# A gated linear recurrence in chunks: the state kept every 64 tokens, with key-value products as 64x64 tiles

## Chip, cores and metric

The kernel runs on one core of a Trainium2 chip. Its time is the device time of one execution in microseconds (us); a run is repeated and the median counts. The engines are named as in the profile: PE (TensorE, matrix products), PEld (its weight loads), DVE (VectorE), ACT (ScalarE), POOL (GpSimd) and SP (SyncE, which issues most transfers).

## What is computed

Two blocks in a row. The first is a recurrence over 768 tokens, for 4 batches and 8 heads of 48 channels; the decay of each step is a complex number per channel. The second mixes the tokens with a product of rank 32 and then applies a two-layer network with a residual.

```python
mag = np.sqrt(a_re * a_re + a_im * a_im)
scale = np.minimum(mag, 0.999) / (mag + 1e-06)
a_re_n, a_im_n = a_re * scale, a_im * scale
for t in range(S):
    new_re = ar * S_re - ai * S_im
    new_im = ar * S_im + ai * S_re
    S_re, S_im = new_re + kv, new_im        # kv: outer product of k and v at t
    y[:, :, t] = einsum('bhd,bhde->bhe', q[:, :, t], S_re)
# x: y as (4, 768, 384)
u = x + (x^T @ U @ V)^T
out = u + np.maximum(u @ w_ch1, 0) @ w_ch2
```

All inputs and outputs are float32.

## The kernel before

The tokens of a batch are cut into 6 chunks of 128 (`CH`), 24 chunks in all. A chunk goes through these stages.

*Gates* (`gates`, L506 to L631), for groups of one or two chunks: the logarithm of the decay's size and its angle, from ACT's functions and some DVE steps. Sums over tokens are products with constant matrices (`es ps` L552, `ph` L610). `totals` (L557) makes the decays over spans of 4 to 128 tokens, and four transfers per group copy them from the tile `E` into the tile `T`, real rows at 0 to 47 and imaginary rows at 48 to 95 (`D2` = 96). `T_of(i, n)` (L633) picks the spans of n tokens.

*Preparation* (`prep`, L639): queries and keys are weighted and turned by their angles into `qkc`, with real and imaginary parts side by side (96 columns a head). PE transposes each head (`tr`, L660) and ACT copies the results into `QK`, so that the 96 channels lie on partitions and the tokens along the row.

*Levels* (`chain`, L668): the product of keys and queries within a chunk is needed with its decay. It is built from small tiles: three rounds of `inner` on blocks of 32 tokens (L694), whose results are kept by mask in `DG` (L700) and placed by four small transfers into the diagonal of `AT` (L731). Between rounds `times` and `grow` (L704, L716) multiply parts of `QK` by the decay of ever longer spans. After `grow` by 16 the `corners` (L743) fill the 32x32 tiles beside the diagonal of each 64 tokens, after `grow` by 32 the `corner` (L760) fills the one 64x64 tile beyond. `AT` is 128 keys by 128 queries a head.

*Rest of a chunk*: `grow` by 64 (L767) brings queries and keys to the edges of the chunk; keys are transposed back into `ks` (L780), except in a batch's last chunk. `outputs` (L789) adds, per head, values times `AT` (L794, all 128 keys deep) and the state `G` of the chunk before times the queries (L798), in a PSUM bank `yT`. `state` (L807) multiplies `ks` by the values (`dk`, L809, one product a head with 96 wide weights); DVE makes the new `G` from the old one, the decay over 128 tokens and `dk` (L813 to L817). `yT` goes through ACT, a transpose `yr` (L824) and ACT again into `xo`.

*Mixing* (`mixer`, L831), two chunks at a time, once all six chunks of the batch are there: `rank`, `mixed`, the first layer `up` (L880) and the second layer `down` (L904, L947).

All operations are handed to a class `Plan` with an engine, an assumed cost, a rank and the buffers they need. `Plan.order` lets them run in a simple model, and the order that comes out is the order of the instructions on each engine. The ranks come from the table `URGENCY` (L25), one number for each kind of work and chunk; smaller goes first, and the mixing goes last where anything else is ready. A `way` marks PE operations that divide the array alike, so that they are kept together. Where PE has nothing to do in the model and no mixing has started, a product without use is issued (`spare`, L1067). The engines run their instructions in order, so a wait on PE holds all that is queued behind it.

PSUM has four pools of two banks: A (`inner`, `corners`, `corner`, `ks ps`), T (sums and `tr`), Y (`yT`, `dk`, `yr`) and M (`up`, `down`). Chunks from the group `PAIRED` = 6 on go through their levels in pairs (`together`, L1009).

## Time and profile before

| | |
|---|---|
| median of 3 runs | 729.14 us (724.9 to 730.22) |
| span of the profiled execution | 722.6 us |
| PE busy | 706.3 us, of which `spare` 57.4 |
| `up`, 864 records | 196.1 us busy |
| `down` by the windows (union of all forms) | 178.1 us |
| VectorE busy | 484.1 us, of which `QK` growths (144) 169.6 |
| ScalarE busy | 399.1 us |
| first `up` starts at | 143.3 us |

How to read it. Times of groups are sums of the durations of their instructions, and matmuls overlap: two that follow each other closely are both counted as busy for part of the same time. The windows view takes the union of the durations, so its sums are lower. What a matmul costs in a row of many is read from the distance of two starts in the timeline. A float32 product leaves two records,[...] and a transpose leaves one. "128*64" after an operation names the rows and columns of the array that it uses, and "128x128" the partitions and columns of the moving operand.

### The profile page before, as it was taken

The page shows a single profiled execution, that of the slowest core. Times are in us where ns is not written, and L with a number is a line of the kernel's source. Part 1 is how long each engine was busy: PE and PEld are TensorE (multiplying, and loading weights), DVE is VectorE, ACT ScalarE, POOL GpSimd, SP SyncE. Part 2 cuts the span into 40 slices and gives each one's busy share as a digit, 9 for nine tenths or more (in the row PEclk, how much of TensorE's full clock was granted, in tenths as well). Part 3 has the DMA queues.
Part 4 walks back from the last instruction along what each step waited for, and adds up shares of the span by engine and source line. Part 5 has one row for each costly group of instructions (what it writes and reads, how often), then busy time and mean ns, then how long its engine had stood idle before and what let it go on. Part 6 is the DMA issues. An engine that isn't in the chain of part 4 may idle for free.

```text
span 722.6 us, 23175 instructions
## 1 busy us (share of the span) xinstructions
PE 706.3 (98%) x10322; PEld 614.7 (85%) x10322; DVE 484.1 (67%) x732; ACT 399.1 (55%) x734; POOL 49.7 (7%) x91
## 2 busy tenths in 40 slices
PE   7899999999999999999999999999999999999998
PEld 7777888786788888978888888798898897989997
DVE  5899999787987958878587685384674741322313
ACT  6696986867789587659988636504314122010010
POOL 5010000010100100000010001000000000000000
PEclk9999999999999999999999999999999999999999
DMA  8787944777415332253441132211110000000000
GB/s 205 154 212 152 214 96 77 172 163 132 100 30 124 67 72 46 44 114 64 86 91 21 26 79 55 46 41 33 35 38 13 15 26 1 22 1 23 6 16 23
DMA packets 165251, 53.00 MB, mean 73 GB/s; under 512 B 154080, under 2 KB 160416, under 8 KB 165152
## 3 DMA queue, kind: packets, MB, share of 16 engines
q1 hardware_dynamic: 161072, 42.26, 27.2%
q0 software_dynamic: 4080, 9.27, 5.6%
q8 instruction: 81, 1.33, 0.8%
q14 instruction: 18, 0.15, 0.1%
HBM read 33.59 MB, written 4.72 MB: 53 GB/s over the span
## 4 chain that ended last, share of the span: by engine, by line
PE 74%; ACT 11%; DVE 10%; issue 2%; DMA 1%; SPq 0%; DVEq 0%; ACTq 0%
PE up L880 21%; PE down L947 19%; PE inner L694 5%; PE tr L660 5%; DVE QK L312 3%; PE yT L794 3%; PE dk L809 3%; ACT x L309 2%; PE down L904 2%; PE yT L798 2%; PE es ps L552 2%; PE mixed L861 2%; PE tot L578 2%; ACT y L309 1%; PE ks ps L780 1%
## 5 line engine op out<-in xcount | busy, mean ns | idle before, releaser
L880 PE MATMUL up<-uT,w 128*128 128x256 f32 x864 | 196.1, 382 | 0.0
L312 DVE TENSOR_TENSOR QK<-QK,T 96x1024 f32<-96x1024 f32 x144 | 169.6, 1186 | 16.7 <-PE corners L743 7.2
L880 PEld LDWEIGHTS up<-uT,w 128*128 128x128 f32 x864 | 161.3, 190 | 22.8 <-issue 0.8
L309 ACT ACTIVATE h<-up 128x512 f32<-128x512 f32 x72 | 42.7, 593 | 158.2 <-PE up L880 155.6
L947 PE MATMUL down<-w,h 128*128 128x192 f32 x396 | 71.8, 327 | 0.0
L947 PEld LDWEIGHTS down<-w,h 128*128 128x128 f32 x396 | 65.2, 190 | 3.3
L312 DVE TENSOR_TENSOR qkc<-qk,cs 128x768 f32<-128x768 f32 x48 | 45.8, 954 | 30.0 <-PE tr L660 24.5
L939 DVE TENSOR_TENSOR stage<-h 128x384 f32<-128x384 f32 x22 | 12.2, 555 | 75.9 <-ACT h L309 75.9
L1067 PE MATMUL spare<-ident 128*128 128x128 f32 x404 | 57.4, 288 | 2.5 <-POOL ident masks.py:199 1.5
L663 ACT COPY QK<-tr 96x512 f32<-96x512 f32 x96 | 52.1, 581 | 13.9 <-PE tr L660 13.7
L694 PEld LDWEIGHTS inner<-QK 96*32 96x32 f32 x4608 | 45.1, 109 | 16.2 <-issue 9.4
L1067 PEld LDWEIGHTS spare<-ident 128*128 128x128 f32 x404 | 51.3, 198 | 5.7 <-issue 1.9
L315 DVE TENSOR_TENSOR xo<-down,xo 128x192 f32<-128x192 f32 (+1 forms) x79 | 29.5, 385 | 38.2 <-PE down L947 38.2
L660 PE MATMUL tr<-ident,qkc 128*96 128x128 f32 x384 | 52.7, 275 | 2.0 <-DVE qkc L312 1.1
L694 PE MATMUL inner<-QK 96*32 96x16 f32 (+1 forms) x4608 | 50.7, 190 | 2.3 <-issue 1.7
L660 PEld LDWEIGHTS tr<-ident,qkc 128*96 128x96 f32 x384 | 41.3, 127 | 8.3 <-issue 1.8
L748 ACT COPY AT<-corners 32x128 f32<-32x128 f32 x96 | 24.5, 255 | 32.1 <-PE corners L743 31.0
L891 POOL DMA_DIRECT2D out_dram<-xo x32 | 17.9, 560 | 335.2 <-DVE xo L315 315.4
L794 PE MATMUL yT<-AT,VP 128*64 128x128 f32 x384 | 36.8, 279 | 0.0
L947 PE MATMUL down<-stage 128*128 128x192 f32 x198 | 36.4, 327 | 0.0
L700 DVE COPY_PREDICATED DG<-mask,inner 128x128 f32<-128x128 int32 (+1 forms) x72 | 24.2, 340 | 17.3 <-PE inner L694 14.0
L306 ACT ACT_TABLE_LOAD x26 | 33.4, 1283 | 1.2 <-PEq L1107 0.7
(116 smaller groups left out, 1106.1 us busy)
## 6 DMA issues: line engine op xcount, KB each, us to landing
stage<-in_moe_w_ch_dram SPq DMA_DIRECT2D x12, 768.0 KB, 5.0
ar<-in_a_re_dram SPq DMA_DIRECT2D x24, 192.0 KB, 3.4
ai<-in_a_im_dram SPq DMA_DIRECT2D x24, 192.0 KB, 3.4
qk<-in_q_dram SPq DMA_DIRECT2D x24, 192.0 KB, 3.8
qk<-in_k_dram SPq DMA_DIRECT2D x24, 192.0 KB, 4.9
VP<-in_v_dram SPq DMA_DIRECT2D x24, 192.0 KB, 3.7
w<-stage POOLq DMA_DIRECT2D x12, 384.0 KB, 7.0
T<-E SPq DMA_DIRECT2D x44, 96.0 KB, 3.0
```

Source lines behind the costliest of these rows:

```text
L306: ACT(1.37, rank, lambda: nc.scalar.preload_act_table_set(name), writes=[TABLE])
L309: return nc.scalar.activation(out=o, in_=i, func=f, **kw)
L312: nc.vector.tensor_tensor(out=o, in0=a, in1=b, op=OP.mult)
L315: nc.vector.tensor_tensor(out=o, in0=a, in1=b, op=OP.add)
L660: nc.tensor.transpose(out=get(*ps)[0:D2, j], in_=get(*qkc)[:, hh * HH + j].rearrange("p u d -> p (u d)"), identity=ident)
L663: ACT(c_act(HH * CH) - 0.05, R1, lambda u=u, hh=hh, ps=ps: nc.scalar.copy(out=get(*QK)[:, u, hh * HH:(hh + 1) * HH], in_=get(*ps)[0:D2]), ...
L694: nc.tensor.matmul(out=get(*ps)[js, h], lhsT=k_of(h)[:, js], rhs=part(q_of(h)[:, js], "p"), start=True, stop=True, tile_position=(0, j * BLK))
L748: ACT(0.32, RR, lambda r=r, u=u: nc.scalar.copy(out=get(*ATi).rearrange("p (a u) t -> p a u t", u=2)[r:r + BLK, :, u, r + BLK:r + 2 * BLK] ...
L794: nc.tensor.matmul(out=a[u * DP:(u + 1) * DP, p], lhsT=vv[:, h], rhs=get(*ATi)[:, h], start=True, stop=(c == 0), tile_position=(0, u * DP))
L880: nc.tensor.matmul(out=get(*ps)[:, e], lhsT=w1[:, f, (ff + e) * 128:(ff + e + 1) * 128], rhs=get(*uT)[:, f], start=(f == 0), stop=(f == KD ...
L947: nc.tensor.matmul(out=get(*to)[:, part], lhsT=x(j), rhs=y[:, j], start=(first and j == 0), stop=(j == KH - 1), skip_group_check=not first)
L1067: nc.tensor.matmul(out=spare[0], lhsT=ident, rhs=ident, start=True, stop=True)
```

## The change

A chunk of 128 tokens now carries its state across two halves of 64 (`HC`). What changes in the work:

- Real and imaginary rows lie 64 partitions apart (at 0 and 64, `DQ` = 112 rows instead of 96), in `QK`, `T`, `ks` and `G`. The rows between are kept at zero in `QKC` and at one in `T`, by memsets at the start. Transposes and their copies take 112 columns or rows.
- `corner` with its two ACT copies and `grow` by 64 are gone. `AT` has 64 columns a head.
- `state` makes the products of keys and values for each half: 64 or 48 wide weights, 64 tokens deep, at the four positions of a 64x64 division of the array, two halves in two PSUM banks `dk`. It also runs in a batch's last chunk, for its first half alone.
- `onward` makes two states a chunk on DVE: the middle one (`GM`) and the end one (`G`).
- `inside` multiplies values and `AT` in each half, again at four positions; `before` adds the state before each half times that half's queries. The two halves of `yT` have a bank each, and two ACT copies.
- The numbers of `URGENCY` are all new.

It does away with the work between the two halves of a chunk, and has the small products share the array.

```diff
 CH = 128
+HC = CH // 2
...
-    D2 = 2 * D
     DP = 64
+    DQ = DP + D
...
+    QKC = singles.tile([128, H, 2, DP], FP, name="QKC")
+    nc.gpsimd.memset(QKC, 0.0)
+    TS = []
+    for n in range(3):
+        TS.append(singles.tile([DQ, GC, H * NTOT], FP, name="T%d" % n))
+        nc.gpsimd.memset(TS[n], 1.0)
...
-        AT.append(singles.tile([128, H, CH], FP, name="AT%d" % n))
+        AT.append(singles.tile([128, H, HC], FP, name="AT%d" % n))
...
-        buffer(QK, "QK", 3, [D2, 2, H, CH])
+        buffer(QK, "QK", 3, [DQ, 2, H, CH])
...
-        ps2 = ("corner", i)
...
-                    nc.tensor.matmul(out=get(*ps2)[u * 64:(u + 1) * 64, p], lhsT=k_of(h)[:, 0:64], rhs=q_of(h)[:, 64:128],
-                                     start=True, stop=True, tile_position=(0, u * 64))
...
-        grow(RR, 64, int(c == 0), 2 - int(c == NCH - 1))
...
+        for r in parts_k:
+            psum(dk[r], "Y", [128, H, D], [128, H, DP])
+
+        def state(h0):
+            for h in range(h0, h0 + HH):
+                for r in parts_k:
+                    at = slice(r * HC, (r + 1) * HC)
+                    for x, end in ((0, DP), (DP, DQ)):
+                        nc.tensor.matmul(out=get(*dk[r])[x:end, h], lhsT=get(*ks)[at, h, x:end], rhs=get(*VPi)[at, h, 0:D],
+                                         start=True, stop=True, tile_position=(r * HC, x))
+        for h0 in (0, HH):
+            PE(0.45, RR, lambda h0=h0: state(h0), [ks, VPi], [dk[r] + (h0,) for r in parts_k], way=3,
+               takes=[mid_G] + ([] if last else [G]))
+
+        def onward(to, of, r):
+            if of is None:
+                DVE(c_dve(DM), RR, lambda: nc.vector.tensor_copy(out=get(*to), in_=get(*dk[r])[0:DQ]), [dk[r]], [to])
+                return
+            DVE(c_dve(DM), RR, lambda: mul(get(*to), get(*of), T_of(i, HC)[:, :, r:r + 1].to_broadcast([DQ, H, D])),
+                [of, ("T", group_of(i))], [to])
+            DVE(c_dve(DM), RR, lambda: add(get(*to), get(*to), get(*dk[r])[0:DQ]), [dk[r]], [to])
+        onward(mid_G, ("G", i - 1) if c else None, 0)
+        if not last:
+            onward(G, mid_G, 1)
...
+        def inside():
+            for p in range(HH):
+                for r in range(2):
+                    for u in range(2):
+                        h, at = 2 * p + u, slice(r * HC, (r + 1) * HC)
+                        nc.tensor.matmul(out=get(*y[r])[u * DP:(u + 1) * DP, p], lhsT=get(*VPi)[at, h], rhs=get(*ATi)[at, h],
+                                         start=(p == 0), stop=(c == 0 and r == 0), tile_position=(r * HC, u * DP),
+                                         skip_group_check=True)
+
+        def before(r):
             for p in range(HH):
                 for u in range(2):
                     h = 2 * p + u
...
+                    nc.tensor.matmul(out=get(*y[r])[u * DP:u * DP + D, p], lhsT=get(*(mid_G if r else ("G", i - 1)))[:, h],
+                                     rhs=q_of(h)[:, r * HC:(r + 1) * HC], start=False, stop=True, tile_position=(0, u * DP),
+                                     skip_group_check=True)
+        PE(0.5, RR, inside, [VPi, ATi, mid_G] + ([("G", i - 1)] if c else []), y, way=3, takes=[yTs])
+        if c:
+            PE(0.45, RR, lambda: before(0), [QK, ("G", i - 1)], [y[0]], way=1)
+        PE(0.45, RR, lambda: before(1), [QK, mid_G], [y[1]], way=1)
+        for r in range(2):
+            ACT(c_act(HH * HC), RR, lambda r=r: nc.scalar.copy(out=get(*yTs)[:, :, r * HC:(r + 1) * HC], in_=get(*y[r])), [y[r]],
+                [yTs + (r,)])
```

More of the change, by code (lines that the diff above doesn't have):

```diff
@@ L25 @@
 URGENCY = {
-    "w1": {0: -34.77, 1: -91.94, 2: 138.23, 3: 260.09, 4: 568.49, 5: 287.6, 6: 296.57},
-    "w2": {0: 650.7, 2: 523.09, 4: -249.29, 6: 129.92, 8: 543.42, 10: 182.29, 12: 94.19},
-    "gates": {0: -78.45, 1: -71.5, 2: 78.63, 4: -234.27, 6: 143.18, 8: 215.64, 10: 30.99, 12: 47.49, 14: 142.08,
-        16: 274.38, 18: 114.7, 20: -16.24, 22: 169.1},
-    "angles": {0: -70.73, 1: -53.23, 2: -131.01, 4: 19.06, 6: -65.31, 8: 37.85, 10: -61.12, 12: -16.54, 14: -136.88,
-        16: -195.15, 18: 196.11, 20: -175.82, 22: 226.2},
@@ L32 @@
-    "prep": {0: -170.41, 1: 140, 2: -141.91, 3: 258.54, 4: -14.67, 5: -36.16, 6: -99.41, 7: -276.32, 8: 64.29,
-        9: 195.98, 10: -226.17, 11: -71.5, 12: -336.86, 13: -82.47, 14: 72.82, 15: -103.91, 16: 99.41, 17: 10.29,
-        18: -125.03, 19: 313.53, 20: -42.62, 21: 390.29, 22: -13.68, 23: -202.37},
-    "levels": {0: 25.49, 1: -241.92, 2: 189.55, 3: -76.47, 4: -144.22, 5: -38.31, 6: -47.77, 7: -81.78, 8: 73.09,
-        9: -35.34, 10: 106.7, 11: -81.83, 12: 144.3, 13: -3.44, 14: 138.61, 15: 149.75, 16: -3.41, 17: -279.49,
-        18: 131.44, 19: 484.09, 20: 212.52, 21: -233.89, 22: -120.03, 23: 283.09},
@@ L38 @@
-    "rest": {0: 147.76, 1: 132.91, 2: 111.2, 3: 94.14, 4: 79.58, 5: 43.3, 6: 213.4, 7: 72.05, 8: 69.08, 9: 53.84,
-        10: 15.71, 11: 8.04, 12: 146.3, 13: 334.57, 14: 62.95, 15: 59.48, 16: -119.25, 17: -34.74, 18: 266.96,
-        19: 135.14, 20: 205.81, 21: 22.53, 22: 320.65, 23: -217.03},
+    "w1": {0: 282.15, 1: -906.54, 2: -637.85, 3: -610.9, 4: 632.97, 5: -937.94, 6: 284.24},
+    "w2": {0: 299.23, 2: 543.83, 4: 718.74, 6: -946.9, 8: -653.99, 10: 454.26, 12: 719.18},
+    "gates": {0: 430.54, 1: 562.72, 2: 181.75, 4: -492.78, 6: 453.57, 8: 425.86, 10: -556.07, 12: 739.21, 14: -629.88,
+        16: 411.04, 18: 334.62, 20: 669.95, 22: -821.66},
@@ new lines @@
+    "angles": {0: 267.44, 1: -865.99, 2: -857.03, 4: -857.13, 6: -1164.36, 8: 397.69, 10: 344, 12: 586.38, 14: 450.22,
+        16: 56.7, 18: 474.46, 20: 559.15, 22: 555.95},
+    "prep": {0: 186, 1: -614.98, 2: -836.46, 3: 718.3, 4: -1006.17, 5: 304.2, 6: -634.69, 7: -700.14, 8: -658.3,
+        9: 457.32, 10: 294.8, 11: -676.14, 12: 261.81, 13: -989.71, 14: -738.32, 15: 456.87, 16: -961.3,
+        17: 412.72, 18: -77.97, 19: -806.53, 20: 253.62, 21: -688.32, 22: -792.69, 23: -735.89},
+    "levels": {0: 604.89, 1: 220.13, 2: -93.4, 3: 34.47, 4: 207.38, 5: 303.07, 6: -786.78, 7: -1203.19, 8: -768.76,
+        9: -959.36, 10: -747.38, 11: 222.7, 12: 555.45, 13: -1005.2, 14: -1116.04, 15: 396.06, 16: 403.94,
+        17: -962.18, 18: 45.03, 19: -928.33, 20: -732.18, 21: 180.02, 22: -835.73, 23: -620.36},
@@ L41 @@
+    "rest": {0: 337.43, 1: -714.43, 2: -760.83, 3: 364.47, 4: -749.7, 5: -993.51, 6: -809.56, 7: 418.33, 8: -764.31,
+        9: -778.02, 10: -1017.5, 11: -814.62, 12: -937.05, 13: 334.88, 14: -665.52, 15: 303.71, 16: 310.56,
+        17: -796.29, 18: -1057.75, 19: -603.28, 20: 315.1, 21: 579.23, 22: -1022.7, 23: -990.48},
 }
@@ L559, in totals @@
             buffer(e, "E", 1, [128, GC, HH, NTOT])
-            buffer(tt, "T", 3, [D2, GC, H * NTOT])
+            ring(tt, "T", TS)
             for i in range(lo, hi):
@@ L565, in totals @@
                     SP(0.65, ("totals", lo), lambda u=u, w=w: nc.sync.dma_start(
-                        out=get(*tt)[u * D:(u + 1) * D, 0:hi - lo, w * HH * NTOT:(w + 1) * HH * NTOT],
+                        out=get(*tt)[u * DP:u * DP + D, 0:hi - lo, w * HH * NTOT:(w + 1) * HH * NTOT],
                         in_=get(*e)[w * 64:w * 64 + D, 0:hi - lo].rearrange("p c h b -> p c (h b)")), [e], [tt + ((u, w),)])
@@ L649, in prep @@
             qkc = ("qkc", 2 * i + u)
-            buffer(qkc, "qkc", 1, [128, H, 2, D])
+            ring(qkc, "qkc", [QKC])
             DVE(c_dve(2 * DM), R1, lambda u=u, qkc=qkc: mul(
-                get(*qkc), get(*qk)[:, u].unsqueeze(2).to_broadcast([128, H, 2, D]), get("cs", g)[:, i - GROUPS[g][0]]),
+                get(*qkc)[:, :, :, 0:D], get(*qk)[:, u].unsqueeze(2).to_broadcast([128, H, 2, D]), get("cs", g)[:, i - GROUPS[g][0]]),
                 [qk, ("cs", g)], [qkc])
@@ L659, in turn @@
                     for j in range(HH):
-                        nc.tensor.transpose(out=get(*ps)[0:D2, j], in_=get(*qkc)[:, hh * HH + j].rearrange("p u d -> p (u d)"),
+                        nc.tensor.transpose(out=get(*ps)[0:DQ, j], in_=get(*qkc)[:, hh * HH + j].rearrange("p u d -> p (u d)")[:, 0:DQ],
                                             identity=ident)
@@ L663, in prep @@
                 ACT(c_act(HH * CH) - 0.05, R1, lambda u=u, hh=hh, ps=ps: nc.scalar.copy(
-                    out=get(*QK)[:, u, hh * HH:(hh + 1) * HH], in_=get(*ps)[0:D2]), [ps], [QK + ((u, hh),)])
+                    out=get(*QK)[:, u, hh * HH:(hh + 1) * HH], in_=get(*ps)[0:DQ]), [ps], [QK + ((u, hh),)])
     def chain(i):
@@ L730, in chain @@
             js = slice(j * BLK, (j + 1) * BLK)
-            SP(0.65, ("place", i), lambda js=js: nc.sync.dma_start(out=get(*ATi)[js, :, js], in_=get(*DGi)[js]), [DGi],
+            to = slice(j % 2 * BLK, j % 2 * BLK + BLK)
+            SP(0.65, ("place", i), lambda js=js, to=to: nc.sync.dma_start(out=get(*ATi)[js, :, to], in_=get(*DGi)[js]), [DGi],
                [ATi + (("d", js.start),)])
@@ L748, in chain @@
                 ACT(0.32, RR, lambda r=r, u=u: nc.scalar.copy(
-                    out=get(*ATi).rearrange("p (a u) t -> p a u t", u=2)[r:r + BLK, :, u, r + BLK:r + 2 * BLK],
+                    out=get(*ATi).rearrange("p (a u) t -> p a u t", u=2)[r:r + BLK, :, u, BLK:2 * BLK],
                     in_=get(*ps1)[r + u * BLK:r + (u + 1) * BLK]), [ps1], [ATi + (("c", r, u),)])
         grow(RR, 32)
-        ps2 = ("corner", i)
-        psum(ps2, "A", [128, HH, 64], [128, H, 64])
-        def corner():
+        G, mid_G, last = ("G", i), ("GM", i), c == NCH - 1
@@ new lines, in chain, with turn @@
+        ks, dk = ("ks", i), [("dk", (i, r)) for r in range(2)]
+        buffer(ks, "ks", 1, [128, H, DQ])
+        buffer(mid_G, "GM", 1, [DQ, H, D])
+        rows_k = HC if last else CH
+        for hh in range(2):
+            ps = ("ks ps", (i, hh))
+            psum(ps, "A", [128, HH, DQ], [128, HH, CH])
+            def turn(hh=hh, ps=ps):
+                for j in range(HH):
+                    nc.tensor.transpose(out=get(*ps)[0:rows_k, j], in_=k_of(hh * HH + j)[:, 0:rows_k], identity=ident[0:DQ, 0:DQ])
+            PE(0.4, RR, turn, [QK], [ps], takes=[ks])
+            ACT(0.54, RR, lambda hh=hh, ps=ps: nc.scalar.copy(out=get(*ks)[0:rows_k, hh * HH:(hh + 1) * HH], in_=get(*ps)[0:rows_k]),
+                [ps], [ks + (hh,)])
@@ new lines, in chain @@
+        if not last:
+            buffer(G, "G", 2, [DQ, H, D])
+        parts_k = range(1 if last else 2)
+        for r in parts_k:
[7 more added lines that the diff above has]
+                                         start=True, stop=True, tile_position=(r * HC, x))
@@ new lines, in chain @@
+        onward(mid_G, ("G", i - 1) if c else None, 0)
+        if not last:
+            onward(G, mid_G, 1)
+        y, yTs = [("yT", (i, r)) for r in range(2)], ("yTs", i)
+        for r in range(2):
+            psum(y[r], "Y", [128, HH, HC], [128, HH, CH])
+        buffer(yTs, "yTs", 1, [128, HH, CH])
+        def inside():
[6 more added lines that the diff above has]
+                                         skip_group_check=True)
@@ L759, in corner @@
                     h = 2 * p + u
-                    nc.tensor.matmul(out=get(*ps2)[u * 64:(u + 1) * 64, p], lhsT=k_of(h)[:, 0:64], rhs=q_of(h)[:, 64:128],
-                                     start=True, stop=True, tile_position=(0, u * 64))
-        yield 0.5, RR, corner, [QK], ps2, ATi
-        for u in range(2):
-            ACT(0.37, RR, lambda u=u: nc.scalar.copy(
-                out=get(*ATi).rearrange("p (a u) t -> p a u t", u=2)[0:64, :, u, 64:128], in_=get(*ps2)[u * 64:(u + 1) * 64]),
-                [ps2], [ATi + (("b", u),)])
@@ L767, in chain @@
-        grow(RR, 64, int(c == 0), 2 - int(c == NCH - 1))
-        G = ("G", i)
-        if c < NCH - 1:
-            ks, dk = ("ks", i), ("dk", i)
-            buffer(ks, "ks", 1, [128, H, D2])
-            buffer(G, "G", 2, [D2, H, D])
-            for hh in range(2):
-                ps = ("ks ps", (i, hh))
-                psum(ps, "A", [128, HH, D2], [128, HH, CH])
-                def turn(hh=hh, ps=ps):
-                    for j in range(HH):
-                        nc.tensor.transpose(out=get(*ps)[:, j], in_=k_of(hh * HH + j), identity=ident[0:D2, 0:D2])
-                PE(0.35, RR, turn, [QK], [ps], takes=[ks])
-                ACT(0.48, RR, lambda hh=hh, ps=ps: nc.scalar.copy(out=get(*ks)[:, hh * HH:(hh + 1) * HH], in_=get(*ps)), [ps],
-                    [ks + (hh,)])
@@ L785, in chain @@
-        y, yTs = ("yT", i), ("yTs", i)
-        psum(y, "Y", [128, HH, CH])
-        buffer(yTs, "yTs", 1, [128, HH, CH])
-        def outputs(p0):
-            a, vv = get(*y), get(*VPi)
-            for p in range(p0, p0 + 2):
-                for u in range(2):
-                    h = 2 * p + u
-                    nc.tensor.matmul(out=a[u * DP:(u + 1) * DP, p], lhsT=vv[:, h], rhs=get(*ATi)[:, h], start=True,
-                                     stop=(c == 0), tile_position=(0, u * DP))
-                for u in range(2 if c > 0 else 0):
-                    h = 2 * p + u
-                    nc.tensor.matmul(out=a[u * DP:u * DP + D, p], lhsT=get("G", i - 1)[:, h], rhs=q_of(h), start=False,
-                                     stop=True, tile_position=(0, u * DP))
@@ L800, in chain @@
-        for p0 in (0, 2):
-            PE(0.95 if c else 0.5, RR, lambda p0=p0: outputs(p0), [VPi, ATi, QK] + ([("G", i - 1)] if c else []), [y + (p0,)], way=1,
-               takes=[yTs])
-        ACT(c_act(HH * CH), RR, lambda: nc.scalar.copy(out=get(*yTs), in_=get(*y)), [y], [yTs])
-        if c < NCH - 1:
-            psum(dk, "Y", [128, H, D], [128, H, DP])
-            def state(h0):
-                for h in range(h0, h0 + HH):
-                    nc.tensor.matmul(out=get(*dk)[0:D2, h], lhsT=get(*ks)[:, h], rhs=get(*VPi)[:, h, 0:D], start=True, stop=True)
-            for h0 in (0, HH):
-                PE(0.68, RR, lambda h0=h0: state(h0), [ks, VPi], [dk + (h0,)], takes=[G])
-            if c == 0:
-                DVE(c_dve(DM), RR, lambda: nc.vector.tensor_copy(out=get(*G), in_=get(*dk)[0:D2]), [dk], [G])
-            else:
-                DVE(c_dve(DM), RR, lambda: mul(get(*G), get("G", i - 1), T_of(i, CH).to_broadcast([D2, H, D])),
-                    [("G", i - 1), ("T", group_of(i))], [G])
-                DVE(c_dve(DM), RR, lambda: add(get(*G), get(*G), get(*dk)[0:D2]), [dk], [G])
+                    nc.tensor.matmul(out=get(*y[r])[u * DP:u * DP + D, p], lhsT=get(*(mid_G if r else ("G", i - 1)))[:, h],
+                                     rhs=q_of(h)[:, r * HC:(r + 1) * HC], start=False, stop=True, tile_position=(0, u * DP),
+                                     skip_group_check=True)
@@ L818, in chain @@
+        PE(0.5, RR, inside, [VPi, ATi, mid_G] + ([("G", i - 1)] if c else []), y, way=3, takes=[yTs])
+        if c:
+            PE(0.45, RR, lambda: before(0), [QK, ("G", i - 1)], [y[0]], way=1)
+        PE(0.45, RR, lambda: before(1), [QK, mid_G], [y[1]], way=1)
+        for r in range(2):
+            ACT(c_act(HH * HC), RR, lambda r=r: nc.scalar.copy(out=get(*yTs)[:, :, r * HC:(r + 1) * HC], in_=get(*y[r])), [y[r]],
+                [yTs + (r,)])
         yr, xi = ("yr", i), ("xo", i)
```

## The prediction

> **What bounds the kernel now.** I read the busy times first and then cut the span into stretches, because one average hides two different phases. In the windows view (columns: stretch, its length, then each engine's busy us with its instruction count, granted clock, DMA share, GB/s) the early rows show VectorE at 38.24 and 39.63 of 40 us, and a late row shows PE at 60.00 of 60 with VectorE at 35.46:

> ```profile
> PE 706.3 (98%) x10322; PEld 614.7 (85%) x10322; DVE 484.1 (67%) x732; ACT 399.1 (55%) x734; POOL 49.7 (7%) x91
> ```

> ```profile
> 40.00:80.00 40.00, 37.47 (x646) 32.25 (x647) 38.24 (x57) 32.56 (x59) 3.78 (x4) 1.00 0.85 189
> 80.00:120.00 40.00, 38.72 (x1042) 32.97 (x1041) 39.63 (x54) 33.48 (x61) 0.86 (x1) 1.00 0.61 121
> ...
> 440.00:500.00 60.00, 60.00 (x936) 51.98 (x937) 35.46 (x52) 24.03 (x57) 3.30 (x5) 1.00 0.21 44
> ```

> The same windows for the tile "spare" (filler matmuls of L1067, which compute nothing) say how much of PE's early business is real:

> ```profile
> 0.00:40.00 40.00, 25.21 (x190) 1.00 0.79 187
> 40.00:80.00 40.00, 15.52 (x106) 1.00 0.85 189
> 80.00:120.00 40.00, 10.59 (x68) 1.00 0.61 121
> 120.00:140.00 20.00, 4.69 (x32) 1.00 0.47 97
> 140.00:200.00 60.00, 1.38 (x8) 1.00 0.66 142
> 200.00:260.00 60.00, 0.00 (x0) 1.00 0.31 67
> ```

> So up to about 143 us, where the first "up" starts, VectorE and ScalarE set the pace and PE has slack; from there to 722.6 us PE is full of useful work. The windows of "yT" hold 176 of 704 records before 140 us, which is the first batch exactly (16 in its first chunk, 32 in each of the other five). Eighteen of the 24 chunks have their tails where PE is the bound, and what PE saves there is saved in the end.

> Prices come from the PE timeline of two neighbouring chunks. A line's second column includes the drain, so I take the difference of two starts:

> ```profile
> 443.41 1.15 PE L760 MATMUL corner<-QK 96*64 96x64 f32 x32
> 444.49 2.86 PE L880 MATMUL up<-uT,w 128*128 128x256 f32 x12
> 447.18 0.83 PE L780 MATMUL ks ps<-ident,QK 96*128 96x96 f32 x8
> 447.94 0.44 PE L794 MATMUL yT<-AT,VP 128*64 128x128 f32 x4
> ...
> 449.85 1.56 PE L809 MATMUL dk<-VP,ks 128*96 128x48 f32 x16
> 451.24 0.62 PE L824 MATMUL yr<-ident,yTs 128*128 128x128 f32 x4
> ...
> 467.72 1.32 PE L694 MATMUL inner<-QK 96*32 96x32 f32 x128
> 468.98 0.55 PE L868 MATMUL uTp<-ident,xo 128*128 128x128 f32 x3
> ```

> A float32 matmul leaves two records, a transpose one. Corner takes 1.08 us for two chunks, 0.54 each; ks 0.76; yT 1.91; dk 1.39. Together 4.60 us a chunk.

> **A pitch for tiled matmuls.** "up" (12 records, 256 columns) takes 2.59 us, 216 ns or 0.84 ns a column. Corner (64 moving columns, 64 wide weights, two column positions) has 54/2 = 27 ns of column time per record; runs of 16 and of 32 records take 0.615 and 1.081 us, so the slope is 29.1 ns and a run costs 0.1 to 0.15 us to enter. Inner (32 columns, four positions: 27/4 = 6.7) takes 0.667 us for 64 and 1.226 for 128: 8.7 ns, entry 0.11. One yT set of four (128 columns, two positions: 53.5) takes 0.22 us: 55 ns. The pitch is thus the column time divided by the positions, plus about 2 ns. dk is limited otherwise: 48 moving columns need 40 ns but a record takes 85 (0.68 us for eight more). [...] So a position is priced at the longer of its load and its stream.

> [...] No row halving is in this trace, so its overlap is unshown here. [...]

> **The change on PE, per chunk.** Removed: corner 0.54, yT 1.91, dk 1.39; ks stays but widens. Added:
> ks: pitch now 82 ns for 96 columns (0.425 us for four, 0.755 for eight), so about 97 for 112: 0.87.
> State: 64 records over four positions, weights 64 and 48 wide, on average 46.7 ns of load: 46.7/4 + 2 = 13.8, times 64, plus entry: 0.98.
> Inside: 32 records at 53.5/4 + 2 = 15.4, plus 0.1: 0.59.
> Before, both halves: 32 records at two positions, 64 columns, like a corner run of 32: 1.06 together, though twice the records of old.
> Sum 3.50, saving 1.10 in a middle chunk. First chunk of a batch: was 0.54 + 0.76 + 0.98 (16 records of yT) + 1.39 = 3.67, becomes 0.87 + 0.98 + 0.59 + 0.59 = 3.03, saving 0.64. Last chunk: had no ks and dk, 0.54 + 1.91 = 2.45; becomes 0.87 + 0.92 (32 state records at 25.5 and entry) + 0.59 + 1.06 = 3.44, costing 1.0. A batch saves 4 x 1.10 + 0.64 - 1.0 = 4.0 us; three batches after 143 us, 12.1 us. If row halves do not overlap, state costs 1.73 and inside 1.03: middle +0.09, first +0.55, last +1.44, a batch +2.35, three of them +7.

> **VectorE.** Gone: the growth by 64, six a batch, four at 1.2 us and two half ones near 0.65 (estimate: half the elements): 6.1. The G updates are 0.55 us apiece:

> ```profile
> L312 DVE TENSOR_TENSOR QK<-QK,T 96x1024 f32<-96x1024 f32 x144 | 169.6, 1186 | 16.7 <-PE corners L743 7.2 <-PE corner L760 6.2 <-PE inner L694 3.2
> L315 DVE TENSOR_TENSOR G<-G,dk 96x384 f32<-96x384 f32 x16 | 8.7, 546 | 10.4 <-PE dk L809 10.4
> ```

> Nine a batch now (one copy, four pairs), twenty-one after (one copy and five pairs for the middle state, five pairs for the end state): +6.6. Net +0.5 a batch; in the first batch it lands on the bound, later it is hidden by PE. Rows 112 instead of 96 deep change nothing, since the time follows the elements in a row.

> **ScalarE.** Two corner copies go (0.366 each); ks copies grow by 64 elements (+0.05 each, at the slope between 581 ns for 512 elements and 366 for 256); one yTs copy of 0.586 becomes two of 0.37. Net -0.47 a chunk, +0.5 in a last chunk: about 7 us less of 399, off the path after 143 us.

> **GpSimd.** One memset of 1024 more for QKC and three for T, 0.945 us each as AT's today, and AT's two halve: +2.9 us ahead of `mid` and `total`. `mid` is done at 6.5 us and its user starts at 9.8, so it fits; `total` slips from 8.9 to about 11.8, against 10.6 for its user. At most 1.2 us, most of it beside VectorE's work on weights. The place copies keep number and size.

> **The new wait.** before(1) and inside need the middle state, which VectorE makes from this chunk's state products; today the old G was ready a chunk ahead. Behind a waiting PE instruction the whole in-order queue stands, "up" and "down" included. And dk and yT now take two Y banks each with only two Y buffers, five uses a chunk for three. The order leaves room for a round trip to VectorE, and today's comparable waits (corners on the growth, 0.4 us in all on PE) are small. I count 0 to 2.4 us a chunk (two growths queued ahead of the add), and take 0.

> Sum: 729.1 - 12.1 + 0.5 (VectorE) + about 0.5 (start) = 718; the urgencies are drawn anew, for which I lean 1 us down: 717.

> **The rivals.** (a) Forecast, row halves overlap and waits are filled: 717, 55 in 100. (b) The new order also brings the first "up" forward. Before 143 us VectorE works on eight chunks' preparation and five groups of gates where batch 0 needs six and four; two preparations of 2.9 us and one gate of about 4.5 could come later. That gives 10 us: 707, 15 in 100. Against it: this work must be done anyway. (c) The round trip or the banks cost about 0.6 us in each of 18 chunks, so nearly all is given back: 727, 18 in 100. (d) Row halves do not overlap, with a small wait on top: 729 + 7 + 2 = 738, 12 in 100, the case on the slower side.

> **How the numbers follow.** 1% is 7.3 us: faster means below 721.8, slower above 736.4. Of (a) I put 0.47 below the first bound and 0.08 within, all of (b) below, of (c) 0.04, 0.12 and 0.02, of (d) 0.03 within and 0.09 above: 0.66, 0.23, 0.11. The range takes in (a), (c) and most of (b) and stops short of (d): 702 to 733.

> **What would show it.** State runs of 64 records in about 1 us and inside runs of 32 in 0.6 (right), or 1.7 and 1.0 (d). PE idle ascribed to VectorE's G line above 5 us would be (c). The first "up" before 138 us would be (b). A first "up" past 150 us, from a poorer order, would prove me wrong in a way I have not priced.

## The result, and the profile after

The changed kernel takes 736.58 us (median of 4 runs, 736.02 to 742.26), the kernel before 728.09 on the same chip (4 runs, 724.9 to 730.22): a measured ratio of 1.0152, interval 1.0104 to 1.02 (the quotient of the two medians is 1.0117, inside that interval). It is slower by one to two per cent, where 717 us and a gain were forecast.

The page of the kernel after, its part on busy time and one line of its DMA queues (packets, MB, share):

```profile
PE 705.4 (96%) x11884; PEld 611.2 (83%) x11884; DVE 488.3 (67%) x756; ACT 392.9 (54%) x718; POOL 52.8 (7%) x95
...
q8 instruction: 93, 1.52, 0.9%
```

PE is busy as long as before (705.4 us against 706.3), but with 1562 more matmul records. The instruction queue line of before was this:

```profile
q8 instruction: 81, 1.33, 0.8%
```

1.52 MB in 93 fetches is 16 KB each. The trace has as many weight loads as matmul records, so PE has about 2 x 11884 instructions, 64 bytes each of the 1.52 MB. By this estimate one fetch holds 256 instructions, or 128 records with their weight loads; before, 81 fetches for 2 x 10322 give 255.

The windows of the kernel after, same columns as before:

```profile
40.00:80.00 40.00, 35.64 (x768) 30.42 (x769) 36.99 (x54) 31.92 (x56) 2.84 (x3) 1.00 0.74 168
80.00:120.00 40.00, 35.63 (x987) 30.60 (x980) 36.67 (x56) 32.03 (x58) 1.71 (x2) 0.98 0.77 165
...
440.00:500.00 60.00, 58.22 (x1150) 50.33 (x1149) 40.33 (x61) 27.32 (x57) 3.94 (x7) 1.00 0.22 49
```

The late rows carry the news. PE had 60.00 of 60 us from 440 to 500; now it has 58.22, and VectorE with 40.33 is not the cause. PE has holes in the phase in which it is the bound. The early rows show VectorE at 36.99 and 36.67 us in place of 38.24 and 39.63, so the first phase is fed less well too.

The PE timeline of a tail in the kernel after (start, duration with drain, line, operation, records) answers the one shown of before:

```profile
455.55 0.93 PE L772 MATMUL ks ps<-ident,QK 112*128 112x112 f32 x8
456.31 2.77 PE L894 MATMUL up<-uT,w 128*128 128x256 f32 x12
459.01 1.14 PE L787 MATMUL dk<-VP,ks 64*64 64x48 f32 x64
460.08 2.86 PE L894 MATMUL up<-uT,w 128*128 128x256 f32 x12
462.78 0.93 PE L772 MATMUL ks ps<-ident,QK 112*64 112x112 f32 x8
463.64 0.69 PE L814 MATMUL yT<-AT,VP 64*64 64x64 f32 x32
464.26 0.65 PE L822 MATMUL yT<-QK,G 112*48 112x64 f32 x16
464.75 0.62 PE L822 MATMUL yT<-QK,GM 112*48 112x64 f32 x16
465.30 0.91 PE L617 MATMUL ph<-z,prefix 128*128 128x384 f32 x2
```

By the distance of two starts: 64 state records take 1.07 us (459.01 to 460.08), 32 inside records 0.62, both halves of `before` 1.04, a `ks` set 0.76 to 0.86. The prices of the prediction were 0.98, 0.59, 1.06 and 0.87. Row halves overlap (without it the state records were priced at 1.73 us and the inside records at 1.03), and the small tiles cost what they should.

Summing PE's time from start to start gives the account. (The 18 chunks after the first `up` are the same work in both kernels.)

| | before | after | difference |
|---|---|---|---|
| start of the first `up` | 143.1 | 156.2 | +13.1 |
| from there to the end | 579.5 | 578.0 | -1.5 |
| of it: corner, dk, ks, yT | 74.9 | 62.4 | -12.5 |
| of it: `inner`, 3456 records in each | 35.6 | 42.5 | +6.9 |
| of it: `up` (+1.6 at half clock, see below) | 190.5 | 193.1 | +2.6 |
| of it: `rank` and `down` | | | +1.5 |

The tail gave 12.5 us, where 12.1 were forecast. But `inner`, whose products have not changed in number or columns, took most of it back, and the first phase grew by 13.1 us.

Where `inner` lost is told by the waits on PE (columns: waiting operation, what ended the wait, total, times, longest), first of before, then of after:

```profile
PE inner L694 <- issue: 1.7, 4, 0.9
```

```profile
PE inner L701 <- issue: 8.6, 8, 1.8
...
PE dk L787 <- issue: 2.4, 1, 2.4
...
PE corners L751 <- issue: 2.0, 2, 1.3
...
PE yT L814 <- issue: 1.4, 2, 0.7
```

"issue" means that nothing the profile shows was waited for: no semaphore, no VectorE line. No wait for G or for a Y bank stands in this list. The timeline around two of these waits in the kernel after:

```profile
430.81 0.69 PE L814 MATMUL yT<-AT,VP 64*64 64x64 f32 x32
431.43 0.65 PE L822 MATMUL yT<-QK,G 112*48 112x64 f32 x16
431.92 0.62 PE L822 MATMUL yT<-QK,GM 112*48 112x64 f32 x16
432.46 1.20 PE L701 MATMUL inner<-QK 112*32 112x16 f32 x120
435.03 0.26 PE L701 MATMUL inner<-QK 112*32 112x16 f32 x8 [1.36 <-issue]
```

```profile
568.71 1.29 PE L701 MATMUL inner<-QK 112*32 112x16 f32 x125
571.78 0.24 PE L701 MATMUL inner<-QK 112*32 112x16 f32 x3 [1.77 <-issue]
571.95 0.76 PE L822 MATMUL yT<-QK,GM 112*48 112x64 f32 x16
```

PE stops in the middle of a run of equal instructions, with 8 or 3 records left, and it does so after a stretch packed with small tiles: in the first case 64 records of the new tail in 1.65 us (430.81 to 432.46, 26 ns each) and then `inner` at about 9 ns a record. Gaps over 0.4 us inside runs of small tiles: in the kernel before one of 1.0 us ahead of the first `up` and one of 0.5 us after it; in the kernel after 7 with 8.2 us and 6 with 7.3 us.

Where do they sit? Count PE's instructions in the trace from its start, weight loads and semaphore instructions included, and take the count modulo 256. All 15 waits of PE for "issue" in the kernel after end at 193 or 194, and so do all 5 in the kernel before. They end 2.2 to 2.9 us after a fetch of the instruction queue began, and no two of these fetches of 16 KB begin less than 3.4 us apart. So a wait for "issue" is read here as a wait for the next block of 256 instructions.

A second loss comes after the first. After the gap before 571.78 the windows show the clock (last but two):

```profile
572.50:576.00 3.50, 3.50 (x13) 2.72 (x10) 3.22 (x5) 0.37 (x1) 0.00 (x0) 0.53 0.02 5
576.00:590.00 14.00, 14.00 (x259) 12.25 (x258) 9.02 (x15) 3.54 (x11) 0.00 (x0) 1.00 0.06 11
```

For 3.5 us the granted clock is 0.53, and `up` runs at 0.43 us a record instead of 0.216. The twelve records from 572.63 take 4.23 us instead of 2.59. The kernel after has three such stretches (from 12.6, 118.4 and 572.4 us), each of 3.41 us at a granted clock of 0.5; the one before has none until its end. In the 3.41 us ahead of the last of them PE stood still for 1.77 us. The first follows a wait of 4.3 us for a mask at the start, the other two follow stops of 2.4 and 1.8 us for a block of instructions; the stop of 1.62 us that ends at 480.56 is followed by none.

The start is late as well. VectorE in the kernel after:

```profile
5.58 3.37 DVE L536 TENSOR_SCALAR x<-x 128x384 f32<-128x384 f32 x1
```

The same step in the kernel before:

```profile
5.64 0.58 DVE L529 TENSOR_SCALAR x<-x 128x384 f32<-128x384 f32 x1
```

GpSimd in the kernel after:

```profile
2.27 0.94 POOL L376 MEMSET QKC<- 128x1024 f32 x1
3.16 2.73 POOL L380 MEMSET T<- 112x1024 f32 x3
5.84 1.45 POOL L383 MEMSET VP<- 128x512 f32 x3
8.43 0.30 POOL L388 MEMSET DG<- 128x256 f32 x1
```

The first VectorE step on the gates lasts 3.37 us, to 8.95; GpSimd's chain of memsets is over at 8.7 us. The next step, ScalarE's logarithm, starts at 9.04 instead of 6.32 us.

That is not all of the first phase's loss. VectorE is its bound, and it has more to do ahead of the first `up` (stretch, length, busy us with count, clock, DMA share, GB/s; first before, then after):

```profile
0.00:143.13 143.13, 125.85 (x186) 1.00 0.72 158
```

```profile
0.00:156.22 156.22, 135.15 (x203) 0.98 0.70 156
```

By the durations of its instructions, the state updates add 6.7 us and the growths that are gone take off 6.1, as forecast. The slowed step adds 2.8. The other 7 us or so are work that stands in both kernels, but ahead of the first `up` in this one: steps on one or two more blocks of weights (4.8) and the first steps of a sixth group of gates (2.4). The new order put them there.

### The profile page after: what moved, and what is told of

Its sections match the earlier page's. It is cut to its first block, busy times and chain, and to the rows that moved or that the text cites. A ratio compares the mean times of both kernels' runs of the same rounds, so it can differ in the third digit from the quotient of the medians.

```text
span 734.3 us, 26344 instructions
## 1 busy us (share of the span) xinstructions
PE 705.4 (96%) x11884; PEld 611.2 (83%) x11884; DVE 488.3 (67%) x756; ACT 392.9 (54%) x718; POOL 52.8 (7%) x95
## 3 DMA queue, kind: packets, MB, share of 16 engines
q8 instruction: 93, 1.52, 0.9%
## 4 chain that ended last, share of the span: by engine, by line
PE 87%; DVE 5%; ACT 4%; issue 3%; DMA 0%; DVEq 0%; ACTq 0%
PE up L894 26%; PE down L961 21%; PE inner L701 6%; PE tr L667 5%; PE dk L787 3%; PE yT L822 3%; PE spare L1081 3%; PE ks ps L772 2%; PE mixed L875 2%; PE down L918 2%; PE ph L617 2%; PE es ps L559 2%; PE yT L814 2%; PE tot L585 2%; PE yr L838 1%
## 5 line engine op out<-in xcount | busy, mean ns | idle before, releaser
L894 PEld LDWEIGHTS up<-uT,w 128*128 128x128 f32 x864 | 162.2, 191 | 24.9 <-issue 1.4
L313 DVE TENSOR_TENSOR QK<-QK,T 112x1024 f32<-112x1024 f32 x120 | 145.3, 1219 | 11.6 <-PE corners L751 8.3
L670 ACT COPY QK<-tr 112x512 f32<-112x512 f32 x96 | 53.3, 591 | 34.2 <-PE tr L667 34.1
L953 DVE TENSOR_TENSOR stage<-h 128x384 f32<-128x384 f32 x22 | 12.3, 558 | 84.3 <-ACT h L310 84.3
L1081 PE MATMUL spare<-ident 128*128 128x128 f32 x462 | 64.5, 288 | 1.4 <-POOL ident masks.py:199 1.4
L701 PEld LDWEIGHTS inner<-QK 112*32 112x32 f32 x4608 | 46.1, 110 | 21.1 <-issue 16.4
L1081 PEld LDWEIGHTS spare<-ident 128*128 128x128 f32 x462 | 58.5, 200 | 4.4 <-POOL ident masks.py:199 1.4
L701 PE MATMUL inner<-QK 112*32 112x16 f32 (+1 forms) x4608 | 52.2, 190 | 8.6 <-issue 8.6
L313 DVE TENSOR_TENSOR QKC<-qk,cs 128x768 f32<-128x768 f32 x48 | 45.8, 954 | 21.5 <-PE tr L667 14.5
L316 DVE TENSOR_TENSOR xo<-down,xo 128x192 f32<-128x192 f32 (+1 forms) x79 | 29.7, 387 | 42.5 <-PE down L961 42.1
L667 PE MATMUL tr<-ident,QKC 128*112 128x128 f32 x384 | 54.3, 279 | 2.4 <-DVE QKC L313 2.1
L667 PEld LDWEIGHTS tr<-ident,QKC 128*112 128x112 f32 x384 | 43.3, 135 | 9.0 <-DVE QKC L313 2.0
L961 PEld LDWEIGHTS down<-stage 128*128 128x128 f32 x198 | 32.5, 190 | 0.6
```

What stands on the lines that cost most here:

```text
L313: nc.vector.tensor_tensor(out=o, in0=a, in1=b, op=OP.mult)
L316: nc.vector.tensor_tensor(out=o, in0=a, in1=b, op=OP.add)
L667: nc.tensor.transpose(out=get(*ps)[0:DQ, j], in_=get(*qkc)[:, hh * HH + j].rearrange("p u d -> p (u d)")[:, 0:DQ], identity=ident)
L670: ACT(c_act(HH * CH) - 0.05, R1, lambda u=u, hh=hh, ps=ps: nc.scalar.copy(out=get(*QK)[:, u, hh * HH:(hh + 1) * HH], in_=get(*ps)[0:DQ]), ...
L701: nc.tensor.matmul(out=get(*ps)[js, h], lhsT=k_of(h)[:, js], rhs=part(q_of(h)[:, js], "p"), start=True, stop=True, tile_position=(0, j * BLK))
L894: nc.tensor.matmul(out=get(*ps)[:, e], lhsT=w1[:, f, (ff + e) * 128:(ff + e + 1) * 128], rhs=get(*uT)[:, f], start=(f == 0), stop=(f == KD ...
```

## The experiments

The leading theory (*supply*): PE's instructions arrive 256 at a time and not faster than every 3.4 us or so, that is 27 ns a record. Work of 9 to 19 ns a record uses instructions up faster than that; the change puts 64x64 products at 17 to 19 ns (1.07 us for 64, 0.62 for 32) next to `inner` at about 9 ns, where products at 55 to 85 ns a record (`yT` and `dk` of before) had left time to fetch. Rivals: the drawn-anew *order* is simply poorer; the *memsets* at the start delay everything; the *wait* for the middle state. In the texts below, each is asked for numbers.

### The two orders exchanged

```diff
 URGENCY = {
-    "w1": {0: 282.15, 1: -906.54, ...   # the changed kernel's
+    "w1": {0: -34.77, 1: -91.94, ...    # the table of the kernel before
...
```

> The changed kernel with the URGENCY table of the kernel before; nothing else differs. Theory S (instruction supply: PE reads its instructions in blocks of 16 KB, 256 instructions, of which one takes at least 3.4 us, and stalls where 128 small matmul records pass in less; the start is 2.7 us late because of the new GpSimd memsets): the kernel's own model of its order ends 15 us later with this table (725.5 against 710.7), and the stalls stay of the same size, so about 745 to 750 us, first 'up' near 168 us, PE stalls at block boundaries of 6 us or more after it. Theory O (the loss comes from the new numbers of URGENCY alone, the change itself is sound): with the old numbers the first 'up' comes back to about 143 us and the time is about 717, as predicted.

Measured: 757.32 us, ratio 1.0458 (1.0409 to 1.0507), first `up` at 175.5 us; gaps in runs of 7.3 us before and 5.1 after it. Theory O is refuted, and the time is also 7 us above the range of theory S.

The same exchange the other way round, the new table in the kernel before:

> The kernel before with the URGENCY table of the changed kernel; nothing else differs. Theory O (the new numbers alone cost the time): first 'up' at about 156 us and the time 735 to 740, the same loss as the whole change. Theory S also expects a slow order here (the model of the order ends at 735.2, first 'up' at 156.1), so the total tells little alone; it expects PE stalls of 1 us or more to stay as few as in the kernel before (4 or fewer, some 4 us in all), since the number of PE instructions is unchanged, and the first DVE tensor_scalar to take 0.6 us and not 3.4.

Measured: 741.76 us against 725.03, ratio 1.0230 (1.0204 to 1.0257), first `up` at 159.0. Gaps: 4.8 us before the first `up` in four places and 1.0 after it in two; a little more than expected.

Each table fits only its own kernel, so these two don't split the loss into "order" and "instructions". They say two things. The new table is not poor for the new instructions: the old one costs 21 us more there. And the late phase of the kernel before stays nearly free of gaps (1.0 us) under either table, that of the changed kernel has 5.1 to 7.3 us under either: the gaps there go with the instructions, not with the table.

### The memsets at the start

```diff
-    nc.gpsimd.memset(QKC, 0.0)
+    nc.vector.memset(QKC, 0.0)
...
-        nc.gpsimd.memset(TS[n], 1.0)
+        nc.vector.memset(TS[n], 1.0)
```

> The changed kernel with the four new memsets (QKC and three T) on VectorE instead of GpSimd. Theory S: GpSimd's memsets held the tensor_scalar of the first gate on VectorE (3.37 us instead of 0.58) and with it the head of the chain; without them it takes 0.6 us, the first 'up' comes about 2.7 us earlier (153.5) and the time falls by 2 to 3 us, to about 734. If VectorE's own memsets wait for GpSimd in the same way, they end near 9 us and nothing is gained (736). Rival (the start is hidden behind later work): no change of the total within 1 us although the first gate comes earlier.

Measured: 734.47 us, ratio 1.0119 (1.0087 to 1.015) against 1.0152 for the change as it was. In the timeline of VectorE the memsets now stand in time that was empty before, and the gate's step is short:

```profile
1.20 0.91 DVE L376 MEMSET QKC<- 128x1024 f32 x1 [0.18 <-issue]
...
5.78 0.43 DVE L536 TENSOR_SCALAR x<-x 128x384 f32<-128x384 f32 x1
```

The first `up` comes at 153.0, 3.2 us earlier. That is a quarter of its delay, and the intervals of the two ratios overlap, so it is read from the trace rather than from the time. The gaps stay: 6.2 and 7.7 us.

### The supply measured by itself

A kernel that runs on PE alone, and leaves out the whole computation: 256 matmuls each (512 records) of `inner`'s kind, of the inside kind and of `before`'s kind, with 24 products of 512 columns between them.

```diff
+    large(24)
+    inner_like(256)     # 128*32, 4 column positions
+    large(24)
+    inside_like(256)    # 64*64, 4 positions
+    large(24)
+    before_like(256)    # 128*64, 2 positions
+    large(24)
```

> Leaves out the whole computation; PE alone, three runs of 256 float32 matmuls (512 records, 1024 instructions) with large matmuls (128x512) between them: 32 wide weights and 32 columns at four column positions as in inner; 64x64 tiles at four positions with 64 columns as in inside; 64 wide at two positions with 64 columns as in before. Theory S: after at most two blocks at full pace, both of the first go at 26 to 28 ns a record (3.4 us for 128), with stalls 256 instructions apart, 13 to 14 us a run; the third, at 29 ns by itself, hardly changes. Rival (no limit on instructions; the stalls in the kernel have another cause): 8.7, 15.4 and 29 ns a record, so 4.5, 7.9 and 15 us.

The PE timeline of this kernel:

```profile
25.06 1.68 PE L84 MATMUL pa<-ident 128*32 128x32 f32 x175
29.18 1.28 PE L84 MATMUL pa<-ident 128*32 128x32 f32 x128 [2.44 <-issue]
32.63 1.93 PE L84 MATMUL pa<-ident 128*32 128x32 f32 x128 [2.17 <-issue]
36.09 1.33 PE L84 MATMUL pa<-ident 128*32 128x32 f32 x81 [1.52 <-issue]
37.34 22.84 PE L79 MATMUL pw<-ident 128*128 128x512 f32 x48
```

and its groups (busy and mean ns, then idle time ahead and its cause):

```profile
L95 PE MATMUL pa<-ident 128*64 128x64 f32 x512 | 15.2, 222 | 0.0
...
L89 PE MATMUL pb<-ident 64*64 64x64 f32 x256 | 8.4, 219 | 3.9 <-issue 3.9
...
L84 PE MATMUL pa<-ident 128*32 128x32 f32 x512 | 6.2, 216 | 6.1 <-issue 6.1
```

No other engine works beside these runs, and no semaphore stands inside one. Still PE stops, 128 records apart once it has begun to, and a block comes every 3.45 us (29.18, 32.63, 36.09; in the inside run 65.00, 68.46, 72.19). At full clock the pitch between the stops is 8.5 ns for `inner`'s kind and 14.7 ns for the inside kind; `before`'s kind, at 29.2 ns, or 3.7 us for 128, is never stopped. The two stopped runs take 12.3 us each, a little less than the 13 to 14 expected, where the rival asked for 4.5 and 7.9. The last two blocks of `inner`'s kind ran at half clock (13.3 and 13.6 ns a record; the page gives a granted clock of 0.5 from 32.7 to 39.9 us), and the distance of the blocks stayed the same, so the pace of the array does not set it here. So the limit is shown directly: 3.4 to 3.5 us for 128 float32 records, 27 ns each, with up to 3.7 us once. After long work the first stop came after 175 records in the one run and after 255 in the other. This kernel ran once.

### The instructions halved where they are densest

If supply is the cause, giving back instructions elsewhere must restore the gain. `inner` takes two heads' queries in one matmul: twice the columns, half the instructions. The products of every other head are left out. It was built on the version with its memsets on VectorE, and on the kernel before, so that what the edit is worth by itself cancels.

```diff
-                for h in range(H):
+                for h in range(0, H, 2):
...
-                        nc.tensor.matmul(out=get(*ps)[js, h], ..., rhs=part(q_of(h)[:, js], "p"), ...
+                        nc.tensor.matmul(out=get(*ps)[js, h:h + 2], ..., rhs=part(get(*QK)[:, 0, h:h + 2, js], "p h"), ...
```

> The kernel after_memset_dve, in which each matmul of inner takes the queries of two heads as its moving side with the keys of the first, so that 32 matmuls a chunk and round become 16 of twice the columns; the products of every other head are therefore left out (other numbers stand in their place). PE's column time stays about the same (by the pitch rule 64 x 15.4 = 0.99 us against 128 x 8.7 = 1.11 us for a pair of chunks), the PE instructions fall by 4608, and the order is unchanged. Theory S (instructions arrive in blocks of 256, at least 3.4 us each): the stalls inside runs fall from 14 us (6.2 before the first 'up', 7.7 after) to 2 or less and the time by 15 to 18 us, to about 718. Rival (stalls have another cause, or the loss lies in the waits for the middle state): the saved column time and entries alone, 3 to 5 us, so about 730, and the stalls stay.

> The kernel before with the same edit of inner (every other head's products left out, half the instructions, same columns). Theory S: this kernel has few stalls to lose (1.5 us inside runs in its profile), so it gains the column time and these, 4 to 7 us, to about 719; the gain must be clearly smaller than the 15 or more of after_wide_inner. Rival: the same 3 to 5 us as there.

Measured: 709.61 us (ratio 0.9779, 0.976 to 0.9797) and 716.25 (0.9875, 0.9859 to 0.9891). Both gained more than expected. Two of the three rounds of `inner` have 16 columns a matmul, and there a record costs as much as with 32 columns (64 records took 0.67 and 0.69 us), so that half as many records shorten the run: a pair's 128 took 1.20 us, the 64 wide ones 0.69. The waits on PE for the changed kernel with wide `inner`:

```profile
PE inner L701 <- issue: 4.5, 3, 2.3
```

(8.1 without it), and in the kernel before with wide `inner` no wait of PE for "issue" is left. The stops in the changed kernel fell from 13.9 to 5.2 us; at most 2 were expected. By phase, from the traces:

| | first `up` | from there to the end |
|---|---|---|
| before | 143.1 | 579.5 |
| before, wide `inner` | 141.1 (-2.0) | 573.4 (-6.1) |
| after, memsets on VectorE | 153.0 | 579.6 |
| after, memsets on VectorE, wide `inner` | 147.6 (-5.4) | 560.6 (-19.0) |

The edit is worth 24.9 us to the changed kernel (734.47 - 709.61) and 9.0 to the kernel before (725.22 - 716.25). The difference of differences is about 16 us, 13 of them after the first `up`. As a price of instruction supply this is an upper estimate. Relieved of work, PE in the kernel before begins to wait for VectorE and ScalarE in the late phase (5.2 us, against 1.1 without the edit), which holds back its gain; the changed kernel does so less (2.2 us, against none). With instructions relieved the changed kernel is the faster one by 6.6 us, and its late phase is shorter by 12.7 us (560.6 against 573.4): that is the forecast gain of the tail.

### An order that knows of the supply

`Plan.order` draws the order from costs that know nothing of fetches. Here each PE operation tells its number of instructions, the model lets a block of 256 arrive no sooner than 3.5 us after the last, the measured costs of the new operations go in, and the urgencies are searched again. The second kernel is the same but for the supply, which its model does not have.

```diff
-                    free[e] = now + ops[n][1] + (self.change if ops[n][7] != ways[e] else 0.0)
+                    wait, fresh = supply(ops[n][1], ops[n][8])      # SUPPLY = 3.5, or 0.0
+                    seen += ops[n][8]
+                    free[e] = now + wait + ops[n][1] + (self.change if ops[n][7] != ways[e] else 0.0)
```

> The changed kernel with its new memsets on VectorE, the assumed costs of state, inside and before set to the measured ones (0.53, 0.6, 0.5 us), and a model of order that knows that PE gets its instructions in blocks of 256, one in 3.5 us at most; the URGENCY numbers are searched again against that model. Theory S: stalls in runs of 3 us or less in all (model 1.1), first 'up' near 150 us, end at about 722 (model 721.6 with measured-like waits; the model was off by -5 for the kernel before and +4 for the changed one), so 717 to 727. If instruction supply is not what costs, it should be no faster than after_blind, by the model without supply even 4 to 6 us slower.

> The same as after_supply with the supply set to zero in the model of order, and the URGENCY numbers searched with as many trials against that blind model (which ends at 715.1, 4 us ahead of after_supply). Theory S: about 13 us of stalls come on top, so some 730 to 736, 8 to 12 us slower than after_supply. Rival (a better order is all that was wanting): 715 to 720, faster than after_supply.

Measured: 729.01 us with the supply in the model (ratio 1.0051, 1.0031 to 1.007), 740.04 without (1.0208, 1.0185 to 1.0232). The waits of `inner`, with and then without:

```profile
PE inner L716 <- issue: 6.2, 4, 2.7
```

```profile
PE inner L716 <- issue: 10.6, 9, 1.7
...
PE dk L802 <- issue: 5.4, 5, 2.0
```

The 11 us between the two were expected, and so was their sign. What wasn't: gaps of 4.5 and 4.7 us remain in the better one (at most 3 were expected), and the two lie 2 and 4 us above their ranges. A likely reason, not tested: an order spreads small tiles among large work only where large work is at hand, and ahead of the first `up` there is little.

### Orders that are robust against where blocks fall

Last, could the changed kernel win with a better order? The search now took the mean over four positions of the block boundary and rewarded an early end, for the changed kernel (twice, the second with supply known to the planner too) and for the kernel before.

```diff
 URGENCY = {
-    'prep': {0: -3704.54, 1: -1489.63, ...    # after_blind's
+    'prep': ...                               # searched anew
...
```

> As after_blind (changed kernel, new memsets on VectorE, measured costs, a model of order that knows nothing of instruction supply), but its URGENCY numbers were searched so that the order, run with one block of 256 instructions in 3.5 us and averaged over four positions of the block boundaries, ends early. The mean there is 723.9. Theory S: 720 to 728, 12 us or more below after_blind's 740, and stalls in runs of 8 us or less against 22.6. If the block boundaries don't matter, it is no better than after_blind.

> The same search from another start and with the supply known to the model of order as well, as in after_supply; the mean over the four positions is 726.1. Theory S: 722 to 730, no slower than after_supply's 729.

> The kernel before, its URGENCY numbers searched in the same way as those of after_spread and with as many trials from its own table; the mean over the four positions is 726.5, against about 727 for its own table. Theory S: 722 to 728; the changed kernel, tuned alike, is at most 3 us faster than this, because supply takes back most of what its array work saves. Rival (the change is sound, only its order was bad): after_spread beats this one by 10 us or more.

Measured: 734.21, 733.35 and 728.22 us against 726.84 (ratios 1.0109, 1.0097 and 1.0020, intervals up to 0.004 on either side). Both forecasts for the changed kernel missed by 3 us or more, that for the kernel before by 0.2. In the first its late phase did shrink, to 572.8 us, 6.7 less than in the kernel before (579.5), and the gaps in it fell from 7.3 to 1.7 us. But 7.5 us of gaps stayed ahead of the first `up`, VectorE waited 7.5 us for `inner` there (3.2 in the kernel after), and the first `up` came at 159.8. The kernel before, searched alike, is 5 to 6 us faster than the changed one. No order that was tried makes the change a gain.

## Why the prediction was wrong, and where it was right

*The bound and the split into phases.* Right. Up to the first `up` VectorE and ScalarE pace the kernel, then PE; the account follows this line.

*The pitch rule and the tail's 12.1 us.* Right for the tail: 12.5 us, with every piece within 0.11 us of its price and errors of both signs. One reading in it was off: `inner`'s pitch was put down to 32 columns, but the runs of 0.667 us for 64 records have 16, and 64 records with 32 columns take 0.694. So at four positions it is not the columns alone that set the 8.7 ns. Rival (d), row halves that don't overlap, is refuted by 1.07 and 0.62 us for the state and inside runs and by 14.7 ns a record in the kernel that runs on PE alone. That row halves overlap was an estimate of the author's, which no trace of before showed; these runs show it. The load in the state's price, 46.7 ns for 56 columns on average, agrees with the trace of before: the records of weight loads lengthen there from 109 ns at 32 columns (`inner`) to 190 at 128 (`up`), 0.84 ns a column, which makes 47 ns for 56.

*The new wait taken as nothing.* Right: PE never waits for G's line, and the Y banks end no wait. A wait on PE does hold what is queued behind it: while `es ps` waited 4.29 us for a mask (until 12.51 us in the kernel after), nothing else ran on PE, and the next `spare` products, which need no new result, came at 15.05. Rival (c) is refuted.

*Rival (b), an earlier first `up`.* Refuted: 156.2 us.

*The sum.* This is the step that failed. It added what each run of instructions costs on the array and had no term for how instructions reach PE. The prediction noted that `before` has "twice the records of old" and counted 64 state and 32 inside records a chunk, but only as column time. At the measured 27 ns a record, any 128 records that run in less than some 3.4 us use instructions up faster than blocks were seen to come; the state, inside and `inner` runs all do. The missing term: after the first `up`, `inner` costs 6.9 us more and `up` 2.6, so 9.5 us by the account and 13 by the wide-`inner` pair; ahead of it about 3.4 by the pair (5.4 less 2.0). That is some 13 to 16 us in all, more than the 12.1 saved. The trace shows the block (16 KB a fetch, stops 128 records apart in the kernel that runs on PE alone) and what passing from one to the next cost: up to 2.4 us. How much can be fetched ahead was not shown beyond this: in the kernel that runs on PE alone 175 and 255 records, 350 and 510 instructions, ran ahead of the first stop, each time after 48 long ones.

*The start.* "It fits" and "about 0.5" was mis-sized. The prediction looked at who reads `mid` and `total`, and there it had slack; it did not look at who works beside the memsets. VectorE's step took 3.37 us instead of 0.58 while they ran. Why, was not shown: the addition just before, which reads two inputs, took its usual 0.56 us beside the same memsets. With the four memsets on VectorE the step took 0.43 us and the first `up` came 3.2 us earlier.

*VectorE's +0.5 a batch and the urgencies' -1.* The first is right for the first batch, the only one where it shows: 6.7 less 6.1 us. The rows cost nothing, as priced: a growth of 1024 elements a row took 1215 ns on 96 rows and 1219 on 112, a state update of 384 elements 546 to 552 and 549 to 556. The second was mis-sized. The order mattered more than a lean of 1 us could hold: with the same computation the times of the changed kernel range from 729.01 to 757.32 us. The prediction named "a first 'up' past 150 us, from a poorer order" as what it had not priced. The first `up` came 13.1 us later: 3.2 us are the memsets' and about 3.4 the supply's. Against the other 6.5 stand the 7 us of weights and gates that the new order puts on VectorE ahead of it. Rival (b) had hoped to move such work out of this phase; the new order moved gates and weights in. No run takes that work away by itself, so this part is read from the trace and not tested. Nor was the cost of the half-clock stretches taken out by itself.

## What to carry to other kernels

Cutting products into smaller tiles saved array time here (12.5 us in the tail), but it left 1562 more matmul records with as many weight loads, in 12 more fetches: beside columns and positions, sum the records. Here, where 128 float32 records took less than some 3.4 us and other such runs stood next to them, the difference had to be paid. The sign in these traces was a PE that stopped inside a run of equal matmuls and waited for "issue" (such gaps: 13.9 us with the memsets on VectorE, 5.2 with wide `inner` as well); packets of the instruction queue against matmul records (93 for 11884) gave the count. When a memset is put on an idle engine, ask not only who needs its result but who works beside it: here a step of 0.58 us took 3.37.
